# Windowed attention and a mish FFN on one core: unsummed weight pieces stored early, merged q, k and v loads, chunk 2's outputs by SyncE and VectorE

## The chip, the cores and the metric

One core of a Trainium2 chip runs the whole program. The metric is the device time of one execution in microseconds (us), as the median of several runs. Engines are named as the profile names them: PE (TensorE), DVE (VectorE), ACT (ScalarE), POOL (GpSimd) and SP (SyncE, which here issues DMAs only).

## The reference

The kernel computes attention with a window of 64 over 8 sequences of 576 positions with 8 heads of 64 (`scale` is 1/8), puts the heads of a token side by side (`x`, 4608 x 512), and applies a feed-forward layer with `w_in` 512 x 2048, the mish function and `w_out` 2048 x 512.

```python
    scores = scale * np.matmul(q, k.transpose(0, 1, 3, 2))
    pos = np.arange(S)
    rel = pos[:, None] - pos[None, :]
    mask = (rel >= 0) & (rel < window)
    scores = np.where(mask, scores, -1000000000.0)
    scores = scores - np.max(scores, axis=-1, keepdims=True)
    attn = np.exp(scores)
    attn = attn / (np.sum(attn, axis=-1, keepdims=True) + 1e-09)
    return np.matmul(attn, v).astype(np.float32)
...
    h = x @ w_in
    sp = np.where(h > 20.0, h, np.log1p(np.exp(np.minimum(h, 20.0))))
    g = h * np.tanh(sp)
    return (g @ w_out).astype(np.float32)
```

## The kernel before

The tokens are cut into 12 chunks of 384. Heads go in 4 pairs. Every fp32 operand of the feed-forward layer is split into a high and a low fp32r part, and a product is three matmuls (high x high, high x low, low x high). The weights stay in SBUF: `wi` for the first layer, `wo_h` and `wo_l` for the second.

Chunks 0 and 1 run interleaved, step by step, while the weights are loaded and split. Their instructions are held in program order, and at the end of that stage the attention of chunk 2 (`third`) is finished beside them: `third.load(p, "v")` loads a pair's values, `third.values` multiplies them. Chunks 2 and 3 then run plainly, one weight column group `f` after the other. From chunk 4 on the kernel works on two chunks at a time (`Wide`, four of them), with a Strassen-Winograd scheme of seven products on 2 x 2 blocks. It needs weight pieces that are sums of blocks. They are made once, beside chunks 2 and 3, for 8 groups `g`:

- `make_sums(g)` (L794 and on) builds four sums in a tile `w` on DVE (L799, one 128x1024 subtract of blocks of `wi`; L803, four more of 128x256), takes their high part `high` on ACT (L805) and their low part on DVE (L807, `w<-w,high`).
- `keep_sums(g)` (L812 and on) stores what the products need in a DRAM tile `sums`: two unsummed pieces (L815, 128x1024; L816, 128x2x256) and the high and low sums (L820 twice). Each is a DMA on SP's queue, and `after_step` makes it wait for the PE step before it. `load_sums` (L824) reads them back on ACT's queue for the products; the home of `wi` is then reused as a ring.

Meanwhile `wides[0].run(k)` (L852) runs the attention of the first two wide chunks: value products of pair k-1, score products of pair k, then `probs` (masks with maxima on DVE, exponentials on ACT, one multiply and one 32x32 transpose for each half on DVE, 12 moves `pT<-tr` on SP's queue), then the loads of the next pair by `after`: q, k and v for each of the two halves, six DMAs. `fills` (L919) prepares the activation blocks of a `Wide`: four POOL subtracts `t1`, `t2`, `b12`, `t2` again (L925), a high copy on ACT (L916) and a low subtract on DVE (L917) for each of the products. In `pair`, `u3` is copied by ACT (L976) and the sums of products `u` and `t` are made on DVE (L969).

Outputs: `ffn_store` and `out_products` call `store_tile` (L379), which copies a PSUM bank to a tile `o` (L383, on ACT or DVE) and stores it (L388). `o` shares a ring of four homes ("pr") with the softmax tiles and the temporaries of `fills`. For chunk 2, ACT copies tiles 0 and 2 and DVE tile 1; SP stores tile 1, ACT the two others.

SP works through its DMAs in order. A DMA also waits until the one eight issues before it on the same semaphore has landed; SP's and ACT's transfers share these semaphores. The order of PE is written out by the program; the other engines' orders come from a scheduler at build time, within the program's dependences.

In the main loop over the steps `n`, chunk 2's value products and loads stand at the end of chunk 1; a pair's products are followed at once by the load of the pair after next into the same home (`values`, L508):

```python
            if last < n < last + NPAIR:
                third.values(n - last - 1, h_bank)
...
            if last - 2 <= n < last:
                third.load(n - last + 2, "v")
```

Of the kernel before, what the change touches and what calls it, by code (L numbers as in the profile page):

```python
# [29 lines left out]
def tile_window_attn_mish_ffn(  # L30
# [89 lines left out]

    wi = const.tile([P, NF, 2, NC_, P], F32R, name="wi")
# [32 lines left out]
    st_turn, v_turn = itertools.cycle(range(3)), itertools.cycle(range(2))  # L154
# [3 lines left out]

    def v_home(shape, name):
        return ap_.tile(shape, F32, name=name, tag=f"v{next(v_turn)}", bufs=1)  # L160
# [6 lines left out]
    def load_qk(c, p):  # L167
# [13 lines left out]
        q_t = ap_.tile([P, width], F32, name="q_t")  # L181
        k_t = ap_.tile([P, width + BLK], F32, name="k_t", bufs=2)
# [7 lines left out]
    def load_v(c, p):  # L190
# [3 lines left out]
        for at, n, tag in parts:  # L194
            shape = [P, n, P]
            v_t = (mp.tile(shape, F32, name="v_t", tag=tag, bufs={"gh": GHS, "gl": GLS}[tag]) if tag else
                   v_home(shape, "v_t"))
# [3 lines left out]
        return tiles  # L201

# [82 lines left out]
    def run_transpose(pr, pT, n=None):  # L285
        shape = [P, TK // TQ, pr.shape[1], TQ]
        tr = v_home(shape, "tr") if n is None else st_home(shape, F32, "tr", n)
        vec.transpose(tr.rearrange("p k j i -> p j k i"), pr.rearrange("p j (k i) -> p j k i", i=32))
        return pT, each_move(pT, tr)
# [189 lines left out]
    class Att:  # L479
# [7 lines left out]
        def load(self, p, what):  # L487
            a = self
            if p >= NPAIR:
                a, p = (self.next, p - NPAIR) if self.c < PLAIN - 1 else (atts[PLAIN + p - NPAIR], 0)  # L490
# [92 lines left out]
    atts = [Att(c) for c in range(NATT)]  # L583
# [197 lines left out]
    def piece(g, m):  # L781

        def at(first, order="p (l k n) -> p l k n"):
            return ring[:, g % 2, first * PIECE:(first + 1) * PIECE].rearrange(order, l=2, k=2)
# [3 lines left out]
        return at({S2: 2, S3: 3, S4: 4, S1: 5, A22: 6}[m])  # L788
# [5 lines left out]
    def make_sums(g):  # L794
# [12 lines left out]
        nc.vector.tensor_tensor(low, w, high.bitcast(F32), ALU.subtract)  # L807
# [415 lines left out]
```

## Time and profile before

| what | value |
|---|---|
| three runs | 916.98, 918.5, 912.92 us; median 916.98 us |
| profiled execution | 912.17 us, of which the span of the profile is 910.4 us |
| mean granted clock of PE over the span | 0.988 of full speed |
| busy: PE, DVE, ACT, POOL | 874.2, 449.3, 458.5, 219.0 us |
| DMA | 152.04 MB, mean 167 GB/s |

Times in the profile are microseconds from the start of the span. A line such as L383 is a line of the kernel before; where a helper records all operations, it has the helper's line (L82 for what is issued in program order, L129 for every matmul). "<-" between two engines means that the first waited and the second released it. In `out<-in` the first name is the tile written. PE clock is the granted share of full speed, 2.4 GHz; the lower level is 1.2 GHz. The DMA share is the mean busy share of 16 DMA engines. Rows of the profiled execution must be held against its own time, 912.17 us.

### The profile page before, as it was taken

The numbers are of one execution on the slowest core, as the hardware profiler recorded it, in microseconds if no ns is written. First come the engines' busy times: TensorE is split into PE (matmuls) and PEld (weight loads), VectorE is DVE, ScalarE is ACT, GpSimd is POOL, SyncE is SP. The second block draws the span as 40 slices with busy tenths as digits, with TensorE's granted clock in tenths as the row PEclk, the third lists the DMA queues.
The fourth block names the chain that finished last, engine by engine and source line by source line (L and its number), as shares of the span: only waits on it lengthen the run. The fifth ranks groups of instructions, "written<-read, shape, count | busy, mean of one in ns | idle before, by whom it ended". The sixth has DMA issues, their size and how long they took to land.

```text
span 910.4 us, 18898 instructions
## 1 busy us (share of the span) xinstructions
PE 874.2 (96%) x7162; PEld 773.5 (85%) x7162; DVE 449.3 (49%) x1279; ACT 458.5 (50%) x1207; POOL 219.0 (24%) x211
## 2 busy tenths in 40 slices
PE   7899999999979998899998999999999999999998
PEld 5798899888868986789887888887898898989996
DVE  7896888123553657433437524528434334322222
ACT  6866574366653664643555634537535435332322
POOL 4400000021211243212243131234122225232221
PEclk9999999999998998999999999999999999999999
DMA  9553444323588884754653755555656343442401
GB/s 301 176 178 131 160 160 130 105 87 90 180 274 268 280 265 138 237 170 154 193 176 122 252 163 162 181 169 173 200 176 205 127 154 117 158 150 85 133 30 70
DMA packets 97914, 152.04 MB, mean 167 GB/s; under 512 B 9760, under 2 KB 80928, under 8 KB 93728
## 3 DMA queue, kind: packets, MB, share of 16 engines
q1 hardware_dynamic: 83712, 84.57, 29.2%
q10 hardware_dynamic: 14112, 66.26, 21.7%
q8 instruction: 57, 0.93, 0.4%
q14 instruction: 33, 0.27, 0.1%
HBM read 114.88 MB, written 24.12 MB: 153 GB/s over the span
## 4 chain that ended last, share of the span: by engine, by line
PE 83%; DMA 5%; DVE 5%; ACT 3%; SPq 2%; issue 1%; POOL 0%; DVEq 0%; POOLq 0%; ACTq 0%
PE acc L129 39%; PE m_ps L129 24%; PE h_ps L129 13%; PE at L129 3%; DMA k_t<-kT 3%; PE s_ps L129 3%; ACT pr L82 2%; DVE wi L917 1%; SPq L82 1%; PE o_ps L129 1%; DMA out<-o 1%; DVE pr L82 1%; DVE sm L82 1%; DMA wi<-sums 1%; ACT xn L875 0%
## 5 line engine op out<-in xcount | busy, mean ns | idle before, releaser
L129 PE MATMUL acc<-wo_h,gh 128*128 128x512 f32 x576 | 227.4, 399 | 6.6 <-ACT o L383 6.6
L129 PE MATMUL m_ps<-wi 128*128 128x384 f32 x1152 | 223.0, 341 | 9.9 <-ACT u L976 4.3
L129 PE MATMUL acc<-wo_l,gh 128*128 128x512 f32 x576 | 227.0, 394 | 0.0
L129 PEld LDWEIGHTS m_ps<-wi 128*128 128x128 f32 x1152 | 204.4, 189 | 24.0 <-DVE u L969 5.9
L129 PE MATMUL acc<-wo_h,gl 128*128 128x512 f32 x576 | 224.3, 392 | 0.0
L957 POOL TENSOR_TENSOR gl<-t,gh 128x384 fp32r<-128x384 f32 x128 | 131.7, 1030 | 383.5 <-PE m_ps L129 123.2
L129 PE MATMUL h_ps<-xh,wi 128*128 128x384 f32 x512 | 144.0, 343 | 2.2 <-DVE mx L82 1.8
L129 PEld LDWEIGHTS acc<-wo_h,gh 128*128 128x128 f32 x576 | 108.7, 189 | 26.0 <-ACT o L383 7.0
L129 PEld LDWEIGHTS acc<-wo_h,gl 128*128 128x128 f32 x576 | 108.7, 189 | 24.5
L129 PEld LDWEIGHTS acc<-wo_l,gh 128*128 128x128 f32 x576 | 108.8, 189 | 15.4
L82 ACT ACTIVATE pr<-pr,mx 128x96 f32<-128x96 f32 (+1 forms) x288 | 105.5, 372 | 19.5 <-DVE mx L82 19.4
L952 ACT ACTIVATE gh<-t 128x384 fp32r<-128x384 f32 x96 | 50.4, 525 | 125.1 <-DVE t L969 86.2
L969 DVE TENSOR_TENSOR u<-u,m_ps 128x384 f32<-128x384 f32 x64 | 35.3, 552 | 134.6 <-PE m_ps L129 134.6
L129 PEld LDWEIGHTS h_ps<-xh,wi 128*128 128x128 f32 x512 | 95.2, 191 | 6.2 <-issue 2.2
L969 DVE TENSOR_TENSOR t<-u,m_ps 128x384 f32<-128x384 f32 x96 | 53.1, 553 | 84.0 <-PE m_ps L129 84.0
L82 DVE CUSTOM_DVE_ANT_0 pr<-s_ps,masks 128x96 f32<-128x96 f32 (+1 forms) x256 | 49.6, 259 | 79.0 <-PE s_ps L129 78.8
L129 PE MATMUL h_ps<-xl,wi 128*128 128x384 f32 x256 | 87.2, 341 | 0.0
L82 POOL TENSOR_TENSOR gl<-t,gh 128x384 fp32r<-128x384 f32 x32 | 34.9, 1090 | 193.8 <-ACT gh L82 187.8
L82 ACT ACTIVATE t<-h_ps 128x384 f32<-128x384 f32 x64 | 31.4, 491 | 58.5 <-PE h_ps L129 56.2
L1042 DVE TENSOR_TENSOR acc_sb<-acc_sb,acc 128x512 f32<-128x512 f32 x56 | 38.4, 686 | 34.8 <-PE acc L129 34.8
L82 ACT ACTIVATION_READ_ACCUMULATOR pr<-pr,mx 128x1 f32 x288 | 55.1, 191 | 0.0
L953 ACT ACTIVATE t<-t 128x384 f32<-128x384 f32 x96 | 50.2, 525 | 8.8 <-PE m_ps L129 0.5
(70 smaller groups left out, 917.8 us busy)
## 6 DMA issues: line engine op xcount, KB each, us to landing
wi<-sums ACTq DMA_DIRECT2D x32, 1024.0 KB, 5.2
wi<-sums ACTq DMA_DIRECT2D x32, 768.0 KB, 4.5
v_t<-vN SPq DMA_DIRECT2D x46, 384.0 KB, 4.9
k_t<-kT SPq DMA_DIRECT2D x44, 224.0 KB, 5.1
pT<-tr SPq DMA_DIRECT2D x192, 48.0 KB, 3.5
q_t<-qT SPq DMA_DIRECT2D x47, 192.0 KB, 5.2
st<-w_in SPq DMA_DIRECT2D x16, 512.0 KB, 3.5
st<-w_out SPq DMA_DIRECT2D x16, 512.0 KB, 3.6
```

Of the source, the lines that this page charges most:

```text
L82: i = call(*args, **kw)
L129: i = nc.tensor.matmul(*args, **kw)
L917: nc.vector.tensor_tensor(low, b, high.bitcast(F32), ALU.subtract)
L952: nc.scalar.activation(gh, t, AF.Mish)
L953: nc.scalar.activation(t, t, AF.Mish)
L957: nc.gpsimd.tensor_tensor(gl, t, gh.bitcast(F32), ALU.subtract)
L969: nc.vector.tensor_tensor(out_, a, b, ALU.add)
L1042: nc.vector.tensor_tensor(total, total, acc, ALU.add)
```

## The change

Six edits, which leave PE's products as they are:

1. `keep_pieces(g, n)` stores the unsummed pieces for all eight groups in the last steps of chunk 1 (two calls in each of two steps): 4 DMAs of two groups each (128x2x1024) and 8 of 128x2x256, on SP's queue. `keep_sums` keeps its two DMAs for the high and the low sums, whose order in `sums` changes so that rows are twice as long.
2. `q_all`, `k_all` and `v_all` are tiles that stay; the former homes of q, k, v and the transposes `tr` of chunks 0 to 3 are parts of them. `wide_qk` and `wide_v` load both halves of a wide run in one q, one k and one v transfer.
3. The low part of the sums is taken on POOL instead of DVE.
4. Chunk 2's tile 2 is copied by DVE instead of ACT, and SP's queue stores all three tiles.
5. `b12 - b11` of `fills` is taken in place on POOL in `run(2)`; `fills` has two POOL subtracts ahead of its first use (`t2`, `t3`) instead of three.
6. A `Wide`'s output tiles 0 and 3 have a home of their own.

```diff
+    q_all = const.tile([P, 2 * CH], F32, name="q_t")
+    k_all = const.tile([P, 2 * (CH + BLK)], F32, name="k_t")
+    v_all = const.tile([P, 2 * NB, P], F32, name="v_t")
...
+    def wide_qk(c, p):
+        base = bases[c]
+        k_t = k_all[:, :2 * CH + BLK]
+        load.dma_start(q_all, qT[p, :, base:base + 2 * CH])
+        load.dma_start(k_t, kT[p, :, base:base + 2 * CH + BLK])
+        return [(q_all[:, u * CH:(u + 1) * CH], lambda rows, n, w, u=u: k_t[rows, u * CH + n:u * CH + n + w]) for u in range(2)]
+
+    def wide_v(c, p):
+        src = vN[p, bases[c]:, :]
+        load.dma_start(v_all, bass.AP(tensor=vN.tensor, offset=src.offset, ap=[[P, P], [BLK * P, 2 * NB], [1, P]]))
+        return [[v_all[:, u * NB + i, :] for i in range(NB)] for u in range(2)]
...
-    def store_tile(row, acc, by, ending=False, queue=None):
+    def store_tile(row, acc, by, ending=False, queue=None, o=None):
         rows = slice(row, row + P)
-        o = ap_.tile([P, DO], F32, name="o", tag="pr", bufs=PRS)
+        if o is None:
+            o = ap_.tile([P, DO], F32, name="o", tag="pr", bufs=PRS)
...
         for t in range(len(acc)):
-            store_tile(bases[c] + t * P, acc[t], nc.scalar.copy if t in (0, 2) else nc.vector.tensor_copy,
-                       queue=nc.sync if c == 2 and t == 1 else None)
+            third_ = c == 2
+            store_tile(bases[c] + t * P, acc[t], nc.scalar.copy if t == 0 or t == 2 and not third_ else nc.vector.tensor_copy,
+                       queue=nc.sync if third_ else None)
...
-        nc.vector.tensor_tensor(low, w, high.bitcast(F32), ALU.subtract)
+        nc.gpsimd.tensor_tensor(low, w, high.bitcast(F32), ALU.subtract)
...
+    def keep_pieces(g, n):
+
+        after_step(nc.sync.dma_start(
+            sums[g:g + n, :, :2 * PIECE].rearrange("g p n -> p g n"),
+            wi[:, 2 * g:2 * (g + n):2].rearrange("p g l c n -> p g (l c n)").bitcast(F32)))
+        for g in range(g, g + n):
+            after_step(nc.sync.dma_start(sums[g, :, 6 * PIECE:].rearrange("p (l n) -> p l n", l=2),
+                                         wi[:, 2 * g + 1, :, 2:, :].rearrange("p l c n -> p l (c n)").bitcast(F32)))
+
     def keep_sums(g):
-
-        f0, f1 = 2 * g, 2 * g + 1
-        after_step(nc.sync.dma_start(sums[g, :, :2 * PIECE], wi[:, f0].rearrange("p l c n -> p (l c n)").bitcast(F32)))
-        after_step(nc.sync.dma_start(sums[g, :, 6 * PIECE:].rearrange("p (l n) -> p l n", l=2),
-                                     wi[:, f1, :, 2:, :].rearrange("p l c n -> p l (c n)").bitcast(F32)))
         for i, part in enumerate(made.pop(g)):
-            to = sums[g, :, 2 * PIECE:6 * PIECE].rearrange("p (m l n) -> p m l n", m=4, l=2)
-            after_step(nc.sync.dma_start(to[:, :, i, :], part.bitcast(F32)))
+            to = sums[g, :, 2 * PIECE:6 * PIECE].rearrange("p (h l n) -> p h l n", h=2, l=2)
+            after_step(nc.sync.dma_start(to[:, :, i, :], part.rearrange("p (h m) n -> p h (m n)", h=2).bitcast(F32)))
...
+                self.load(k, "v")
+                if k == 2:
+                    b11, b12 = (self.block(0, j) for j in range(2))
+                    nc.gpsimd.tensor_tensor(b12, b12, b11, ALU.subtract)
...
-            t1, t2 = temp("t1"), temp("t2")
-            sub(t1, b12, b11)
+            t2, t3 = temp("t2"), temp("t3")
             sub(t2, b22, t1)
-            sub(b12, b22, b12)
+            sub(t3, t2, b11)
...
+                if t in (0, 3) and "o" not in self.homes:
+                    self.homes["o"] = st_home([P, 2, DO], F32, "o", 1)
...
+        early_pieces = starts[2] // 2 - 3 - n
+        if early_pieces in (0, 1):
+            for g in (0, 2):
+                keep_pieces(4 * (1 - early_pieces) + g, 2)
```

Two places of the order are shown. The first is SP's queue in the last steps of chunk 1, from the last transposed moves of chunk 2 (`pT`) to the first q and k loads of chunk 3; `v_t` are value loads, of chunk 2's pairs 0 to 3 first. Before:

```order
79 L82 DMA pT<-tr 32x192 x12
80 L82 DMA v_t<-vN 128x6x128 x6
81 L82 DMA q_t<-qT 128x384
82 L82 DMA k_t<-kT 128x448
83 L82 DMA pT<-tr 32x192 x12
```

The same place of SP's queue after the change:

```order
79 L82 DMA pT<-v_t 32x192 x12
80 L82 DMA v_t<-vN 128x6x128
81 L838 DMA sums<-wi 128x2x1024
82 L82 DMA v_t<-vN 128x6x128
83 L842 DMA sums<-wi 128x2x256 x2
84 L838 DMA sums<-wi 128x2x1024
85 L842 DMA sums<-wi 128x2x256 x2
86 L838 DMA sums<-wi 128x2x1024
87 L842 DMA sums<-wi 128x2x256 x2
88 L838 DMA sums<-wi 128x2x1024
89 L842 DMA sums<-wi 128x2x256 x2
90 L82 DMA v_t<-vN 128x6x128 x4
```

Twelve stores of unsummed pieces have come between the value loads: pairs 0 and 1 of chunk 2 keep their place, apart from one store, and pairs 2 and 3 stand behind all twelve. (In this listing `tr` has the name `v_t` after the change where it is part of `v_all`.)

The second place is DVE around run 1 of the first `Wide`: the end of run 0 (multiply and transpose), the sums of one group, and the first masks of run 1. Before:

```order
430 L82 TENSOR_TENSOR pr<-pr,sm 128x576
431 L82 STREAM_TRANSPOSE tr<-pr 128x6x3x32
432 L799 TENSOR_TENSOR w<-wi 128x2x2x256
433 L803 TENSOR_TENSOR w<-w 128x256 x4
434 L807 TENSOR_TENSOR w<-w,high 128x1024
435 L82 ISA pr,mx<-s_ps,masks 128x96
436 L82 ISA mx 128x1
```

The same place of DVE after the change:

```order
429 L82 TENSOR_TENSOR pr<-pr,sm 128x576
430 L82 STREAM_TRANSPOSE tr<-pr 128x6x3x32
431 L823 TENSOR_TENSOR w<-wi 128x2x2x256
432 L827 TENSOR_TENSOR w<-w 128x256 x4
433 L823 TENSOR_TENSOR w<-wi 128x2x2x256
434 L82 ISA pr,mx<-s_ps,masks 128x96
435 L82 ISA mx 128x1
```

The low part (L807) has left DVE, and the next group's first subtract (L823, L799 before), which stood behind run 1's masks and the copy of an output tile, has moved ahead of the masks.

## Rows read from the trace of the kernel before

**Rows 1.** Page, part 1: busy us (share of the span) x instructions of each engine.

```profile
PE 874.2 (96%) x7162; PEld 773.5 (85%) x7162; DVE 449.3 (49%) x1279; ACT 458.5 (50%) x1207; POOL 219.0 (24%) x211
```

**Rows 2.** Waits of PE, 225 to 400 us: us in total, times, longest us.

```profile
PE acc L129 <- ACT o L383: 6.6, 1, 6.6
PE m_ps L129 <- ACT u L976: 4.3, 2, 3.2
PE h_ps L129 <- DVE mx L82: 1.8, 1, 1.8
...
PE m_ps L129 <- DVE mx L82: 1.0, 1, 1.0
PE at L129 <- DMA out<-o: 0.9, 1, 0.9
PE at L129 <- DMA pT<-tr: 0.6, 1, 0.6
```

**Rows 3.** Waits of PE, 400 to 910 us, the same columns.

```profile
PE m_ps L129 <- DVE u L969: 3.3, 5, 0.9
PE m_ps L129 <- DVE t L969: 3.0, 2, 1.5
```

**Rows 4.** Windows of 10 us: us; busy PE, PEld, DVE, ACT, POOL; clock, DMA share, GB/s.

```profile
160.00:170.00 10.00, 10.00 (x89) 8.76 (x89) 2.74 (x5) 3.15 (x7) 0.00 (x0) 1.00 0.39 125
...
260.00:270.00 10.00, 6.65 (x87) 5.51 (x75) 5.32 (x31) 5.64 (x27) 0.00 (x0) 1.00 1.06 359
270.00:280.00 10.00, 6.76 (x23) 6.19 (x24) 4.46 (x9) 4.45 (x7) 1.22 (x2) 0.66 0.75 256
...
290.00:300.00 10.00, 8.18 (x35) 6.97 (x32) 6.95 (x34) 9.10 (x30) 0.00 (x0) 0.83 1.06 367
...
350.00:360.00 10.00, 6.74 (x20) 5.43 (x19) 7.17 (x7) 2.18 (x4) 3.66 (x3) 0.66 0.29 89
```

**Rows 5.** Timeline of SP, 255 to 276 us: start, us, what it issues.

```profile
258.00 0.71 SPq L820 DMA_DIRECT2D sums<-w  x1
```

**Rows 6.** Timeline of DVE, 250 to 276 us: start, us, instruction, idle before, releaser.

```profile
260.72 0.26 DVE L82 CUSTOM_DVE_ANT_0 pr<-s_ps,masks 128x96 f32<-128x96 f32 x1 [3.46 <-PE s_ps L129]
...
267.50 1.23 DVE L799 TENSOR_TENSOR w<-wi 128x1024 f32<-128x1024 f32 x1 [3.96 <-DMA sums<-w]
```

**Rows 7.** Timeline of ACT, 155 to 186 us, the same columns.

```profile
156.02 0.49 ACT L82 ACTIVATE t<-h_ps 128x384 f32<-128x384 f32 x1 [1.44 <-PE h_ps L129]
```

**Rows 8.** Timeline of PE, 140 to 200 us, values of chunk 2's pair 2.

```profile
170.55 0.92 PE L129 MATMUL o_ps<-pT,v_t 128*64 128x64 f32 x24
```

**Rows 9.** Windows of 5 us, columns as in rows 4.

```profile
295.00:300.00 5.00, 5.00 (x19) 4.51 (x18) 3.14 (x11) 4.97 (x22) 0.00 (x0) 0.66 1.08 396
...
315.00:320.00 5.00, 5.00 (x26) 4.50 (x25) 5.00 (x25) 4.42 (x18) 0.00 (x0) 1.00 1.02 319
```

**Rows 10.** DMA issues, 145 to 200 us: KB each, median us to landing.

```profile
v_t<-vN SPq DMA_DIRECT2D x6, 384.0 KB, 3.4
```

**Rows 11.** Timeline of ACT, 262 to 275 us: start, us, instruction, idle before, releaser.

```profile
270.54 1.28 ACT L82 ACT_TABLE_LOAD   x1 [3.87 <-DMA v_t<-vN]
...
272.59 0.59 ACT L383 COPY o<-acc 128x512 f32<-128x512 f32 x1
```

**Rows 12.** POOL's instructions by line and form: busy us, mean ns; idle before.

```profile
L925 POOL TENSOR_TENSOR t<-xn 128x768 f32<-128x768 f32 x4 | 7.3, 1827 | 0.0
```

**Rows 13.** Timeline of ACT, 345 to 377 us.

```profile
353.82 0.48 ACT L976 COPY u<-m_ps 128x384 f32<-128x384 f32 x1 [1.77 <-DVE w L807]
```

**Rows 14.** Timeline of DVE, 338 to 377 us.

```profile
349.40 2.41 DVE L82 TENSOR_TENSOR pr<-pr,sm 128x576 f32<-128x576 f32 x1
351.73 2.02 DVE L807 TENSOR_TENSOR w<-w,high 128x1024 fp32r<-128x1024 f32 x1
...
373.58 0.76 DVE L82 TENSOR_TENSOR pr<-pr,sm 128x576 f32<-128x576 f32 x1
```

**Rows 15.** Timeline of POOL, 336 to 377 us.

```profile
348.62 2.56 POOL L925 TENSOR_TENSOR t<-xn,t 128x768 f32<-128x768 f32 x1 [1.63 <-DVE wi L917]
```

More of the change, by code (lines that the diff above doesn't have):

```diff
@@ L152, in at_set @@
         return ps_at.tile([P, DO], F32, name=name, tag=f"at{n}")
-    st_turn, v_turn = itertools.cycle(range(3)), itertools.cycle(range(2))
+    st_turn, q_turn, v_turn = (itertools.cycle(range(n)) for n in (3, 2, 2))
     def st_home(shape, dtype, name, n=None):
         return mp.tile(shape, dtype, name=name, tag=f"st{next(st_turn) if n is None else n}", bufs=1)
-    def v_home(shape, name):
-        return ap_.tile(shape, F32, name=name, tag=f"v{next(v_turn)}", bufs=1)
     def in_steps(c, p):
@@ L180, in load_qk @@
             return q_t, keys
-        q_t = ap_.tile([P, width], F32, name="q_t")
-        k_t = ap_.tile([P, width + BLK], F32, name="k_t", bufs=2)
+        i = next(q_turn)
+        q_t = q_all[:, i * CH:(i + 1) * CH]
+        k_t = k_all[:, i * (CH + BLK):(i + 1) * (CH + BLK)]
         first = c == 0 and p < 2
@@ L195, in load_v @@
             shape = [P, n, P]
-            v_t = (mp.tile(shape, F32, name="v_t", tag=tag, bufs={"gh": GHS, "gl": GLS}[tag]) if tag else
-                   v_home(shape, "v_t"))
+            if tag:
+                v_t = mp.tile(shape, F32, name="v_t", tag=tag, bufs={"gh": GHS, "gl": GLS}[tag])
+            else:
+                i = next(v_turn)
+                v_t = v_all[:, i * NB:(i + 1) * NB, :]
             load.dma_start(v_t, bass.AP(tensor=vN.tensor, offset=src.offset + at * BLK * P,
@@ L489, in load @@
             if p >= NPAIR:
-                a, p = (self.next, p - NPAIR) if self.c < PLAIN - 1 else (atts[PLAIN + p - NPAIR], 0)
+                a, p = self.next, p - NPAIR
+                if self.c == PLAIN - 1:
+                    if p == 1:
+                        wides[0].load(0, what)
+                    return
             if a:
@@ L581, in tile_window_attn_mish_ffn @@
     steps += [(c, f) for c in range(2, PLAIN) for f in range(NF)]
-    atts = [Att(c) for c in range(NATT)]
+    atts = [Att(c) for c in range(PLAIN)]
     for a, b in zip(atts, atts[1:]):
@@ L787, in piece @@
             return both[:, :, m == A12]
-        return at({S2: 2, S3: 3, S4: 4, S1: 5, A22: 6}[m])
+        if m == A22:
+            return ring[:, g % 2, 6 * PIECE:].rearrange("p (l k n) -> p l k n", l=2, k=2)
+        i = (S2, S3, S4, S1).index(m)
+        two = ring[:, g % 2, (2 + i // 2 * 2) * PIECE:(4 + i // 2 * 2) * PIECE]
+        return two.rearrange("p (l m k n) -> p l m k n", l=2, m=2, k=2)[:, :, i % 2]
     def after_step(i):
@@ L856, in run @@
             if k >= 1:
-                for u, a in enumerate(self.atts):
-                    value_products(a.v[k - 1], a.pT.pop(k - 1), [at[u][:, n:n + BLK] for n in range(0, CH, BLK)])
+                moves = self.pT.pop(k - 1)
+                for u in range(2):
+                    value_products(self.v[k - 1][u], (pT_all[:, :, u], moves), [at[u][:, n:n + BLK] for n in range(0, CH, BLK)])
             if scored:
@@ L861, in run @@
                 s_ps = {}
-                for u, a in enumerate(scored.atts):
+                for u in range(2):
                     for m in range(NM):
@@ L900, in probs, with load @@
                                                 tr[r:r + TQ, i].rearrange("p u j q -> p (u j q)")))
-            for u, a in enumerate(self.atts):
-                a.pT[k] = pT_all[:, :, u], moves
-                self.after(u, k, "qk")
-        def after(self, u, k, what):
-            if k + 1 < NPAIR:
-                self.atts[u].load(k + 1, what)
-            elif self.next:
-                self.next.atts[u].load(0, what)
+            self.pT[k] = moves
+            self.load(k + 1, "qk")
+        def load(self, k, what):
+            a, k = (self, k) if k < NPAIR else (self.next, 0)
+            if a:
+                getattr(a, what)[k] = {"qk": wide_qk, "v": wide_v}[what](a.cs[0], k)
         def block(self, i, j):
```

22 lines of the change are left out of this document (10 added, 12 removed).

## The prediction

> **What bounds the kernel now.** I read the page first, then PE's waits, then the timelines around each wait. PE is busy for 96% of the span [rows 1], so only two things can move the time: stretches in which PE stands still, and stretches in which it runs at the lower of its two clock levels. The change removes no matmul. The waits between 225 and 400 us [rows 2] sum to some 15 us, and the longest is 6.6 us, for ACT's copy of an output tile. Behind 400 us some 6 us more are spent in front of `m_ps` [rows 3].
>
> The clock adds to it. Between 270 and 280 us the granted clock was 0.66, between 290 and 300 us 0.83, between 350 and 360 us 0.66 [rows 4], each time just behind a stall. A mean of 0.66 is 68% of the time at the half level (1.2 instead of 2.4 GHz): 0.68 x 6.76 us busy = 4.6 us at half speed, 2.3 us lost. By the same working 290 to 300 us lost 0.34 x 8.18 / 2 = 1.4 us, and 350 to 360 us 2.3 us. So a stall of several us costs about 2 us more than its length.
>
> **The early pieces: a new wait.** Twelve stores now stand on SP's queue at the end of chunk 1: 4 of 1.05 MB and 8 of 0.26 MB, 6.29 MB. Before, SP issued the six value loads of chunks 2 and 3 there with nothing between them. Now the loads of pairs 2 and 3 of chunk 2 stand behind all twelve stores. DMA engines have time in that stretch, since their share was 0.39 between 160 and 170 us [rows 4]. But one queue moves its bytes in order: the store of `w` issued at 258.00 us released VectorE only at 267.50 us [rows 5, 6], with other stores and a part of the loads ahead of it.
>
> PE takes pair 2's values at 170.55 us [rows 8]. The first store waits for a step of PE that ends at about 156 us, where ACT takes its `h_ps` [rows 7], so bytes start to move at about 157 us. Up to and including pair 2's load stand 6.29 + 2 x 0.39 = 7.07 MB, and 7.86 MB if chunk 0's three output tiles (0.26 MB each, ACT's queue) share the engines before it. Engines that were full moved 319 to 396 GB/s [rows 9], and 359 GB/s over 260 to 270 us [rows 4]. The fixed part of a landing is 3.4 us [rows 10] less 1.3 us for 0.39 MB at 300 GB/s, 2.1 us. Best: 157 + 7.07/0.396 + 2.1 = 177.0 us, a stall of 6.4 us. Worst: 157 + 7.86/0.319 + 2.1 = 183.7 us, 13.2 us. At 359 GB/s it is 8.3 us without and 10.5 us with the outputs ahead; I take 9.0. Such a stall brought 2.3 us of half clock at 270 us. **Cost: 11.3 us (8 to 16).** What queues behind it: the next activations on ACT stand behind output transfers that wait for stores to land, and PE's steps behind them, but those transfers wait no longer than pair 2's values do, so I count nothing more.
>
> In exchange SP is spared 16 stores between 242 and 332 us, and the six loads at each wide run become three. I count that inside the waits below, since no row shows SP itself holding PE there except 0.6 us at the transposed moves [rows 2].
>
> **Chunk 2's outputs: the 6.6 us.** ACT stood behind its output transfer until `v_t` had landed, 3.87 us, then loaded a table (1.28 us) and copied two activations before it reached the third tile at 272.59 us [rows 11]. Now SP stores, and VectorE copies the third tile, behind one multiply and one transpose, each some 0.76 us [rows 14], after the last exponential (270.54 - 3.87 = 266.67 us [rows 11]). The copy ends at about 268.9 us, so a stall of about 2.2 us stays: gain 4.4 us. A stall that short at 292 us still brought 1.4 us of half clock, so I count 1.2 of the 2.3 us. Against that, VectorE's next piece sum (`w<-wi`) now stands ahead of run 1's masks and waits for the store of the last sum, as it waited 3.96 us in before, behind them [rows 6]. The masks began at 260.72 us. That store was issued at 258.00 us [rows 5]; with POOL's longer subtract (below) it is issued some 1.2 us later, and lands, at the 3.4 us of rows 10, at 262.3 to 262.6 us if less stands ahead of it. With the sum's own 1.23 us the masks are late by 0 to 3.1 us; I take 1.0 us for PE. Net gain 4.6 us (minus 3.1 to 8.9).
>
> **The low part of the sums on POOL.** It takes 1.23 us of VectorE eight times; on POOL the nearest row is 1.83 us for 768 columns [rows 12], so 1024 columns take about 2.4 us. VectorE is freed ahead of run 2's masks, where PE waited 1.8 us [rows 2] and lost 1.4 us of clock: I take 2.4 of these 3.2 us (0 to 3.2).
>
> At the change to the first `Wide`, ACT's `u` copy waited for VectorE's subtract [rows 13], whose tile shares the home, and PE waited for `u`. The subtract ran from 351.73 us and took 2.02 us [rows 14], since it stood behind a multiply stretched by POOL. On POOL it would end at about 352.2 us. That stretch holds 6.2 us of waits (4.3 for `u`, 1.0 for `mx`, 0.9 for `out<-o`) [rows 2] and 2.3 us of half clock. I take 4.0 us (0 to 8.5).
>
> POOL's work beside VectorE has a price that speaks against this part: a multiply of 0.76 us took 2.41 us beside POOL's subtract [rows 14, 15], 1.65 us more, and POOL's own took 2.56 instead of 1.83 us. The Trainium skill (SBUF — State Buffer, section "Who interferes with whom") says that a VectorE operation with two SBUF inputs and a GpSimd operation that reads SBUF exclude each other, and that the later of the two waits until the first is done. The trace agrees: the multiply that began at 349.40 us ended at 351.81 us, 0.63 us after POOL's subtract ended at 351.18 us. By that rule each moved subtract can hold VectorE for up to its own length; by the row alone the price is 1.65 us a collision. It is rival 2.
>
> **Fills and the own output home.** Each fill has one POOL subtract fewer (1.83 us) at its start, and tiles 0 and 3 no longer wait for a home of the softmax ring. The waits in the three later transitions sum to 6.3 us [rows 3], of which I take about half, 3.3 us (0 to 6.3).
>
> **Sum.** Gains 4.6 + 2.4 + 4.0 + 3.3 = 14.3 us; cost 11.3 us; net minus 3.0 us. The profiled execution took 912.17 us (span 910.4), so 909.2 us; it lies 4.8 us under the median of the three runs, 916.98, so against that median I expect 914 us. By the ends of the terms the net goes from minus 18 (all 26.9 us of gains, the least cost, 8.4 us of which 6.4 are the stall and 2.0 its clock) to plus 19 (no gain, masks 3.1 us late, 15.5 us of cost).
>
> **Rivals.**
> 1. *The value loads are not late.* If loads pass the stores, or the stores drain before 170 us, only the gains stay: minus 14.3 us, 903 us. For it: engines at 0.39 share [rows 4]. Against it: 7.07 MB in the 11.5 us from 157 to 168.5 us would need 615 GB/s, and no full stretch shows over 396 [rows 9].
> 2. *POOL against VectorE, slower.* The eight subtracts fall beside the multiplies of runs 0 to 4, and the chain masks, exponentials, multiply, transposes, moves gets later. Once already PE waited for its end (0.6 us for `pT<-tr` [rows 2]), so there is little slack. One collision in each of four runs costs 1.65 us and some 1.5 us of half clock: 12.6 us on top of minus 3.0, plus 9.6 us, 927 us. It decides from a slack under 1.65 us. Against it: POOL is free most of that stretch, and VectorE gets 1.23 us back a sum.
> 3. *The gains do not come.* Another wait of the same run ends as late as the removed one (the table load, the moves, the masks), and only a third of the gains is left: 11.3 - 4.8 = plus 6.5 us, 923 us. For it: the chains of ACT and VectorE in 260 to 275 us are long whatever the copy does. Against it: the 3.87 us on ACT are spent on nothing but a transfer [rows 11].
>
> **How the numbers follow.** Forecast 0.42, rival 1 0.25, rival 2 0.17, rival 3 0.16. The forecast's own range is 908 to 921. About 1% (9.2 us) is what a measurement of this kernel can tell from no change. Faster by more: nearly all of rival 1 and a little of the forecast, 0.31. Slower by more (over 926): two thirds of rival 2, some of rival 3 and the forecast's tail, 0.19. The rest, 0.50, is within 1%. The range that leaves out one in ten on either side is 899 to 927 us.
>
> **What would show it.** Right: a new wait of PE in front of chunk 2's `o_ps` at about 170 us, of 6 to 13 us, released by `v_t<-vN`; a granted clock near 0.66 behind it; the 6.6 us at 266 us down to 2 or 3; no wait for `u` over 2 us near 351 us; waits before `m_ps` behind 400 us at about half. Wrong: no wait at 170 us (rival 1), new waits on `pT<-tr` or `mx` between 250 and 335 us with VectorE's multiplies over 2 us (rival 2), or the wait at 266 us still over 5 us, with another releaser (rival 3).

## The result and the profile after

The changed kernel took 925.95 us (median of 12 runs, 919.96 to 930.8) against 915.52 us for the kernel before (12 runs, 912.71 to 919.68): a ratio of 1.011, with a 95% interval of 1.0081 to 1.014. It is slower by some 10 us. The forecast was 914 us, a little faster than before; the time lies inside the stated range (899 to 927 us), but on the other side of no change.

The profiled execution took 927.89 us (span 926.1 us, mean granted clock 0.980, against 910.4 us and 0.988). The waits of PE between 165 and 235 us in the changed kernel, in the columns of [rows 2] (before, that stretch has none):

```profile
PE o_ps L132 <- issue: 9.7, 1, 9.7
```

And its waits of PE between 235 and 405 us, the largest and the least:

```profile
PE at L132 <- issue: 5.6, 1, 5.6
PE m_ps L132 <- ACT u L1005: 4.4, 2, 3.1
PE h_ps L132 <- DVE mx L82: 3.5, 1, 3.5
PE m_ps L132 <- DVE u L998: 1.1, 1, 1.1
...
PE at L132 <- DMA pT<-tr: 0.3, 1, 0.3
```

"issue" as a releaser means that the profile shows nothing that the engine waited for. The wait of 6.6 us for the output tile [rows 2] is gone. But 9.7 us have come in front of chunk 2's values (`o_ps`), 5.6 us in front of run 2's values (`at`), and the wait for `mx` has grown from 1.8 to 3.5 us; the wait for `u` is as long as it was. All waits of this view sum to 18.7 us between 235 and 405 us; in the kernel before it was 16.4 us. Behind 405 us they sum to 4.8 us instead of 6.3 us [rows 3]:

```profile
PE m_ps L132 <- DVE t L998: 3.1, 2, 1.6
PE m_ps L132 <- DVE u L998: 1.2, 2, 0.6
PE m_ps L132 <- ACT u L1005: 0.5, 2, 0.3
```

The windows of 10 us around the new wait, columns as in [rows 4], show the engines of the DMA full and the clock falling:

```profile
160.00:170.00 10.00, 10.00 (x89) 8.59 (x88) 2.74 (x5) 3.14 (x7) 0.00 (x0) 1.00 1.04 375
170.00:180.00 10.00, 0.87 (x6) 0.55 (x4) 0.56 (x1) 1.46 (x3) 0.00 (x0) 0.77 1.03 340
180.00:190.00 10.00, 9.40 (x72) 7.80 (x73) 1.12 (x2) 0.96 (x2) 0.00 (x0) 0.72 0.34 104
```

Over 165 to 235 us the mean clock was 0.93 with PE busy for 60.28 us, so 0.07 x 60.28 = 4.2 us were lost; before it was 1.00 there. The two profiled spans differ by 15.7 us. The parts are 9.7 us of new wait, 4.2 us of clock behind it, 2.3 us more waits and 1.4 us more half clock between 235 and 405 us, less 1.5 us of waits behind that and 0.5 us at the start. The clock is given to two digits, so each part that comes from it is known to within about 1 us. The medians differ by 10.4 us: the profiled execution of before, 912.17 us, is near the low end of its runs, that of after in the upper half of its own.

### The profile page after: what moved, and what is told of

Same layout as the page of the kernel before. It is cut to its first block, busy times and chain, and to the rows that moved or that the text cites. A ratio compares the mean times of both kernels' runs of the same rounds, so it can differ in the third digit from the quotient of the medians.

```text
span 926.1 us, 18789 instructions
## 1 busy us (share of the span) xinstructions
PE 879.9 (95%) x7162; PEld 777.8 (84%) x7162; DVE 444.0 (48%) x1272; ACT 458.4 (50%) x1206; POOL 238.9 (26%) x219
## 5 line engine op out<-in xcount | busy, mean ns | idle before, releaser
L132 PEld LDWEIGHTS acc<-wo_h,gh 128*128 128x128 f32 x576 | 109.1, 190 | 19.5 <-issue 0.3
L132 PEld LDWEIGHTS acc<-wo_l,gh 128*128 128x128 f32 x576 | 109.6, 190 | 15.7
```

Source lines behind the costliest of these rows:

```text
L132: i = nc.tensor.matmul(*args, **kw)
```

## Where the new wait comes from

SP's timeline of the changed kernel, 150 to 200 us, from the third of the large stores on:

```profile
163.55 1.25 SPq L838 DMA_DIRECT2D sums<-wi  x1
164.84 2.53 SPq L842 DMA_DIRECT2D sums<-wi  x2
167.42 1.29 SPq L838 DMA_DIRECT2D sums<-wi  x1
168.76 2.58 SPq L842 DMA_DIRECT2D sums<-wi  x2
171.43 15.84 SPq L82 DMA_DIRECT2D v_t<-vN  x4
```

PE's timeline there, the first product after the wait:

```profile
180.59 1.55 PE L132 MATMUL o_ps<-pT,v_t 128*64 128x64 f32 x24 [9.72 <-issue]
```

SP reached pair 2's value load only at 171.43 us, when the last store was issued. The view of DMA issues (KB each, us to landing) for 171.4 to 172 us shows how long that load then took:

```profile
v_t<-vN SPq DMA_DIRECT2D x1, 384.0 KB, 9.0
```

So the values were there at 180.6 us, within the bounds of the prediction's working (177 to 184 us). Whether the stores are the cause, and whether it is their place in the queue or the load on the engines, four kernels tell.

**e1: the early stores undone.** The pieces are stored again by `keep_sums`; all else is as changed.

```diff
     def keep_sums(g):
+        f0, f1 = 2 * g, 2 * g + 1
+        after_step(nc.sync.dma_start(sums[g, :, :2 * PIECE], wi[:, f0].rearrange("p l c n -> p (l c n)").bitcast(F32)))
+        after_step(nc.sync.dma_start(sums[g, :, 6 * PIECE:].rearrange("p (l n) -> p l n", l=2),
+                                     wi[:, f1, :, 2:, :].rearrange("p l c n -> p l (c n)").bitcast(F32)))
...
-        if early_pieces in (0, 1):
-            for g in (0, 2):
-                keep_pieces(4 * (1 - early_pieces) + g, 2)
```

> The changed kernel with its early pieces undone: the unsummed pieces are stored again in keep_sums, between 242 and 332 us; all else as changed. Theory (the stores on SP's queue make chunk 2's values late): the 9.7 us wait in front of o_ps and its half clock go, 12 us less than the changed kernel's 925.95, so 914 us or a little more, since 6.3 MB come back beside the wide runs. Rival (POOL's subtracts and VectorE's collisions cost the time, and the stall at 170 us is made good later): under 4 us less, 922 us or more.

Measured: 911.43 us, 0.9938 of before (0.9916 to 0.996), and no wait of PE between 100 and 235 us. So the early stores cost 14.5 us by the medians, and what is left of the change (the other five edits and the new order of rows in `sums`) is a gain of about 0.6%. The theory holds; the rival falls.

**e2: the same stores in chunk 2.**

```diff
-        early_pieces = starts[2] // 2 - 3 - n
-        if early_pieces in (0, 1):
-            for g in (0, 2):
-                keep_pieces(4 * (1 - early_pieces) + g, 2)
+        late_pieces = n - starts[2] // 2 - 1
+        if late_pieces in (0, 2, 4, 6):
+            keep_pieces(late_pieces, 2)
```

> The changed kernel with the early pieces stored in the first steps of chunk 2 (behind all value loads, one call in every second step) instead of at the end of chunk 1. Theory: the wait in front of o_ps is gone and nothing comes back beside the wide runs, 12 us less than the changed kernel, 912 to 914 us; the waits of 3.5 us (mx) and 5.6 us (at) between 270 and 310 us stay. Rival (the stores cost wherever they stand): a new wait of 3 us or more in chunk 2, and no more than 6 us less than the changed kernel.

Measured: 917.77 us (909.96 to 921.49), 0.9996 (0.9964 to 1.0028). The 9.7 us are gone; 2.6 us of waits stand in chunk 2 in their place (1.9 us, released by nothing the profile shows, and 0.7 us for `tr`). Its runs scatter over 11.5 us, those of e1 over 2, and the median lies between the two expectations. The trace is that of the fastest run, 909.96 us, so the waits of the slower ones are not seen; what makes them scatter was not found.

**f1: the same stores at the same steps, on POOL's queue.**

```diff
-        after_step(nc.sync.dma_start(
+        after_step(nc.gpsimd.dma_start(
...
-            after_step(nc.sync.dma_start(sums[g, :, 6 * PIECE:].rearrange("p (l n) -> p l n", l=2),
+            after_step(nc.gpsimd.dma_start(sums[g, :, 6 * PIECE:].rearrange("p (l n) -> p l n", l=2),
```

> The changed kernel with the twelve early stores at the same steps, but issued on POOL's queue instead of SP's. Theory (pair 2's values are late because they stand behind the stores in one queue): the loads share the engines packet by packet and pass most of the stores, the 9.7 us wait in front of o_ps falls under 4 us, and the time is 6 us or more below the changed kernel's 925.95. Rival (the DMA engines as a whole are too slow for 6.3 MB there, whatever the queue): a wait of 7 us or more stays and the time is within 4 us of the changed kernel.

Measured: 910.46 us, 0.9958 (0.9937 to 0.9979), no wait between 100 and 235 us. Its windows of 10 us, columns as above:

```profile
160.00:170.00 10.00, 10.00 (x89) 8.59 (x88) 2.75 (x5) 3.15 (x7) 3.28 (x5) 1.00 1.02 349
170.00:180.00 10.00, 10.00 (x90) 8.58 (x89) 1.59 (x3) 3.02 (x7) 3.26 (x5) 1.00 1.06 368
```

Its PE timeline, pair 2's values:

```profile
170.85 0.92 PE L132 MATMUL o_ps<-pT,v_t 128*64 128x64 f32 x24
```

SP's timeline in it, 160 to 162 us, the load of pair 2's values, and the DMA issues of the same stretch:

```profile
161.34 0.37 SPq L82 DMA_DIRECT2D v_t<-vN  x1
```

```profile
v_t<-vN SPq DMA_DIRECT2D x1, 384.0 KB, 4.6
```

The DMA engines were as full as in the changed kernel (349 and 368 GB/s against 375 and 340), and pair 2's values were in time. So it is the place behind the stores in one queue that made them late, not the load on the engines: worth some 15 us of 926.

The delay has two parts. SP issued the load at 161.34 us here and at 171.43 us in the changed kernel, 10.1 us later, because SP first had to issue the stores, which took it 0.9 to 1.3 us each, where a load alone took 0.37 us. Once issued, the load took 9.0 us to land instead of 4.6 us. The Trainium skill (DMA: Bandwidth & Descriptors, section "Queues, rings and completion order") says that each DMA engine takes the entries of one queue in order and takes turns between the queues by packets. The second part agrees with that; it does not explain the first. The Trainium skill (DMA: Bandwidth & Descriptors, section "Rules for kernel authors") says that spreading transfers over the issuing engines does not help bandwidth and only saves time of issuing. The first part agrees with that: the rate hardly changed, and the load was issued 10.1 us earlier. f1 takes away both parts at once, so no run shows which of them alone would have made PE wait. It also spread the stores out, since POOL issued the last of them at 178.30 us and SP by 171.3 us.

**f2: half of the stores early, half in chunk 2.**

```diff
         if early_pieces in (0, 1):
-            for g in (0, 2):
-                keep_pieces(4 * (1 - early_pieces) + g, 2)
+            keep_pieces(2 * (1 - early_pieces), 2)
+        if early_pieces in (-4, -6):
+            keep_pieces(-early_pieces, 2)
```

> The changed kernel with half of the early stores (groups 0 to 3, 3.15 MB) at the end of chunk 1 and the other half in chunk 2. Theory: 3.15 MB less ahead of pair 2's values are 8.8 us at the 359 GB/s of a full stretch, so the 9.7 us wait falls to about 1 us (0 to 3), and the time to that of e2_pieces_late, 918 us or below. Rival (a wait that does not go by bytes but by the queue's waits for landings): 5 us or more of the wait stay.

Measured: 911.22 us, 0.9961 (0.9934 to 0.9987), no wait between 100 and 235 us. SP issued pair 2's load 7.2 us after the first store (15.2 us in the changed kernel), and it took 6.0 us to land (9.0 us): 11 us earlier, where the theory had 8.8 us from the bytes. The wait goes by how much stands ahead; since half the bytes are also half the stores, f2 does not tell the two apart.

## Where the gains went

**e3: chunk 2's outputs alone, in the kernel before.**

```diff
-            store_tile(bases[c] + t * P, acc[t], nc.scalar.copy if t in (0, 2) else nc.vector.tensor_copy,
-                       queue=nc.sync if c == 2 and t == 1 else None)
+            third_ = c == 2
+            store_tile(bases[c] + t * P, acc[t], nc.scalar.copy if t == 0 or t == 2 and not third_ else nc.vector.tensor_copy,
+                       queue=nc.sync if third_ else None)
```

> The kernel before with the edit on chunk 2's outputs alone (VectorE copies tile 2, SP stores all three). Theory (the chain from run 1's masks to the last move is longer than PE's work up to run 2, and the 6.6 us wait only covered that): the wait for o falls to 2 or 3 us, a wait of 3 to 5 us for the moves or masks of run 2 comes in its place, and the time is within 3 us of before. Rival (the wait is lost time, as the prediction took it): 5 to 8 us faster than before.

Measured: 916.76 us, 1.0006 (0.9984 to 1.0027): nothing. The time is the theory's, and so is the new wait for the moves (4.5 us), but the wait for `o` did not shrink; it only has another releaser. PE's waits of 235 to 405 us in this kernel:

```profile
PE acc L129 <- DVE o L383: 6.6, 1, 6.6
PE at L129 <- DMA pT<-tr: 4.5, 1, 4.5
PE h_ps L129 <- DVE mx L82: 2.4, 1, 2.4
```

VectorE's timeline in it, 255 to 276 us:

```profile
267.57 1.23 DVE L800 TENSOR_TENSOR w<-wi 128x1024 f32<-128x1024 f32 x1 [4.06 <-DMA sums<-w]
268.72 0.16 DVE L82 TENSOR_SCALAR sm<-sm 128x6 f32<-128x6 f32 x1
...
272.45 0.68 DVE L383 COPY o<-acc 128x512 f32<-128x512 f32 x1
```

VectorE stood until 267.57 us in front of the first subtract of the next group's sum, waiting for the store of the last sum's low part to land, as it did before (267.50 us [rows 6]). The copy of `o` came behind it in VectorE's order, at 272.45 us; ACT's copy had come at 272.59 us [rows 11]. So ACT's 3.87 us behind the output transfer and VectorE's 3.96 us behind the store were two waits side by side, on two chains that reach the copy of `o` within 0.14 us of each other, and taking one away showed the other.

In the changed kernel the scheduler had moved that subtract ahead of run 1's masks. VectorE's timeline there:

```profile
276.35 1.23 DVE L823 TENSOR_TENSOR w<-wi 128x1024 f32<-128x1024 f32 x1 [10.25 <-DMA sums<-w]
...
284.95 2.51 DVE L82 TENSOR_TENSOR pr<-pr,sm 128x576 f32<-128x576 f32 x1
```

PE's timeline of the changed kernel, the two products behind its waits:

```profile
278.94 0.66 PE L132 MATMUL h_ps<-xh,wi 128*128 128x384 f32 x1 [3.50 <-DVE mx L82]
...
302.89 2.83 PE L132 MATMUL at<-pT,v_t 128*64 128x64 f32 x48 [5.57 <-issue]
```

The last score of run 1 was done at 273.15 us, but VectorE waited for a landing until 276.35 us (10.25 us idle), and PE, which needs the banks that the masks read, stood for 3.5 us. The masks' lateness and a multiply of 2.51 us beside POOL's subtract (284.44 to 286.83 us) then held back the moves, which SP issued from 288.30 to 296.73 us. The 5.6 us in front of run 2's values came at their end. The DMA issues of 296.5 to 297 us show it, a reload of pieces, a store and the last move:

```profile
wi<-sums ACTq DMA_DIRECT2D x1, 1024.0 KB, 6.3
sums<-w SPq DMA_DIRECT2D x1, 512.0 KB, 7.0
pT<-tr SPq DMA_DIRECT2D x1, 48.0 KB, 6.6
```

The moves issued between 294 and 296 us landed in 1.9 us; the last one, beside the reload of 1 MB, took 6.6 us, to about 302.7 us, and PE went on at 302.89 us. Seven more kernels looked at that chain. A measure of it is the interval from the last score of run 1 to the first value product of run 2, and the same from run 2 to 3. In the kernel before they are 26.3 and 21.4 us, in the changed one 29.7 and 21.5 us; from run 0 to 1 of the kernel before, where PE never waits, it is 17.6 us.

**e5: the masks first.** As e2, and the first subtract of the third, fifth and seventh group waits for its run's last mask.

```diff
+        if g % 2 == 0 and "mask" in made:
+            tc.add_manual_dep(first.ins, made["mask"].name, SYNC, reason="masks first")
...
-    sums_at = [(begin + k // 2 * every + (-3, 1, 1, 5)[i + k % 2 * 2], fn, k)
+    sums_at = [(begin + k // 2 * every + (0 if k else -3, 1, 1, 5)[i + k % 2 * 2], fn, k)
```

> As e2_pieces_late, and the first subtract of the third, fifth and seventh group's sums is made to stand behind the masks of its run. Theory: the 3.5 us wait for mx goes, and the 5.6 us wait in front of run 2's values shrinks, as the masks' lateness (3.5 us) was part of it: 4 to 8 us less than e2_pieces_late. Rival (POOL beside the multiply and the reload of pieces beside the moves make that wait): the mx wait goes but the at wait stays at 5 us or more, 2 to 4 us less.

Measured: 912.61 us (910.38 to 913.98), 0.9966 (0.9946 to 0.9986); intervals 24.0 and 22.4 us. No wait for `mx` in front of `h_ps`, but 4.2 us for `o`, since the subtract now stands ahead of that copy, and 2.9 us for `pT<-tr`. By the medians 5.2 us less than e2; with e2's scatter this is weak evidence. **g3: the same on f1.** The diff is that of e5, on f1's early stores on POOL's queue.

> f1_pool_queue (early stores on POOL's queue) with the masks ahead of the next sum as in e5_masks_first. If the two do not touch each other: the 4.3 us wait for mx of f1_pool_queue goes, 2 to 4 us less than its 910.5 us. If the wait only changes its place: within 2 us of it.

Measured: 910.41 us, 0.9943 (0.9925 to 0.9962), against 910.46 us for f1. The 4.3 us for `mx` of f1 are gone and 4.6 us for `o` have come: the wait changed its place.

**f4: no wait for the landing.** e1, with the transfer of the low sums reading unsummed weights (the low parts are left out of the sums).

```diff
-        for i, part in enumerate(made.pop(g)):
+        high, _ = made.pop(g)
+        for i, part in enumerate((high, wi[:, f1].rearrange("p l c n -> p (l c) n").rearrange("p (m a) n -> p m (a n)", m=4))):
```

> e1_pieces_back, where the transfer that stored the low sums reads the unsummed weights instead (same bytes; the low parts in the sums are left out), so that the next group's first subtract no longer waits for a store to land. Theory: that wait held VectorE, and behind it the copy of chunk 2's output tile: the 6.5 us wait for o falls to 3 us or less and the time by 3 to 7 us under e1_pieces_back's 911.4 us. Rival (run 1's own chain of exponentials, multiply and transposes is as long): the wait stays over 5 us, or comes back in front of run 2's values, and the time is within 2 us.

Measured: 912.22 us, 0.9978 (0.9961 to 0.9994), against 911.43 us for e1. The wait for `o` is gone altogether, 6.5 us in e1, and the time did not fall. PE's waits of 235 to 405 us:

```profile
PE s_ps L132 <- ACT gh L82: 8.8, 2, 5.1
PE at L132 <- DMA sums<-wi: 4.0, 1, 4.0
PE at L132 <- DMA pT<-tr: 1.9, 1, 1.9
```

The first interval is 29.3 us, longer than e1's 25.9 us. The time is the one that the expectation's rival gave, but not its mechanism (run 1's own chain of exponentials, multiply and transposes): VectorE finished run 1's transposes at 269.3 us, early, but SP issued the moves from 274.19 us on and took 11.13 us for them (8.43 us in the changed kernel's run 1). The larger part of the wait for `gh` (5.1 of 8.8 us) hangs on the same moves. ACT's timeline, 268 to 290 us:

```profile
284.88 0.49 ACT L82 ACTIVATE t<-h_ps 128x384 f32<-128x384 f32 x1 [6.74 <-DMA pT<-tr]
```

ACT stood 6.74 us until moves had landed; it issued a reload of pieces at 284.45 us, just before it went on, and PE waited 5.1 us for what ACT wrote next.

**g1: no sums' work at all.** e1, with `make_sums` empty and both transfers of `keep_sums` reading unsummed weights. The sums are left out; the bytes and their places stay.

```diff
     def make_sums(g):
-        f0, f1 = 2 * g, 2 * g + 1
...
+        pass
```

> e1_pieces_back without the work of the sums on VectorE, ACT and POOL: keep_sums stores unsummed weights in their place (the same bytes at the same places of SP's queue; the sums are left out). It parts what the engines' sums cost from what their stores cost. Between run 1's last score and run 2's first value lie 17.6 us of PE's own work; in the kernel before that interval is 26.3 us, in e1_pieces_back 25.9 us, and from run 2 to run 3 it is 21.4 and 21.2 us. If the work on VectorE, ACT and POOL holds the chain: both intervals fall to 17.6 to 19 us and the time to 900 us or less. If the stores do (landings, SP's queue): the intervals stay over 21 us, the time at 907 us or more.

Measured: 909.22 us, 0.9937 (0.9915 to 0.9958); intervals 29.3 and 19.4 us. VectorE, ACT and POOL are free of the sums, and run 2's values are 9.7 us late nonetheless. SP's timeline of 262 to 300 us, the moves:

```profile
272.22 11.86 SPq L82 DMA_DIRECT2D pT<-tr  x12
```

The DMA issues of that stretch in g1 (KB each, median us to landing):

```profile
sums<-wi SPq DMA_DIRECT2D x9, 512.0 KB, 7.7
...
k_t<-kT SPq DMA_DIRECT2D x2, 416.0 KB, 6.5
...
pT<-tr SPq DMA_DIRECT2D x12, 48.0 KB, 5.7
```

The moves are 48 KB each and took 5.7 us to land, and 11.86 us to issue, behind 512 KB stores and loads that took 6 to 8 us. The last transpose had ended at 269.7 us.

**g2: neither sums nor stores.** As g1, with all stores in the first steps of chunk 2 (the sums are left out).

```diff
+        if late_pieces in (1, 3, 5, 7):
+            for g in (late_pieces - 1, late_pieces):
...
+                    after_step(nc.sync.dma_start(to[:, :, i, :], part.rearrange("p (h m) n -> p h (m n)", h=2).bitcast(F32)))
...
     def keep_sums(g):
...
+        pass
```

> As g1_no_sums_work, with all stores (pieces and what stands for the sums) moved to the first steps of chunk 2, so that beside the wide runs neither the sums' work nor their stores stand. If the runs' own chain (masks, exponentials, multiply, transposes, moves) is the bound: waits of 5 us or more stay between run 1 and run 3. If the sums and their traffic are: both intervals at 17.6 to 18.5 us, the waits between 235 and 405 us under 5 us, and the time 12 us or more below the kernel before, 902 us or less.

Measured: 921.82 us, 1.0066 (1.0046 to 1.0086). The time says nothing of the runs, because the 14.7 MB of stores, now all in chunk 2, made 12.6 us of waits for moves there (`pT<-tr`), the same fault at another place. The intervals do: 24.3 us from run 1 to 2, still, but 17.4 us from run 2 to 3 and 17.8 us from run 3 to 4. So without the sums and their stores PE never waits between runs 2 and 4. Between runs 1 and 2 it waits once, 3.5 us for `o`, and VectorE's timeline there (276 to 300 us) shows why:

```profile
292.65 0.69 DVE L400 COPY o<-acc 128x512 f32<-128x512 f32 x1 [2.94 <-DMA out<-o]
```

VectorE's copy of the third output tile waited until an earlier output had been stored. PE's clock over that interval was 0.86 with 20.76 us busy, so 2.9 us more were lost. Together that is 6.4 of the 6.9 us by which the first interval exceeds the second.

**h1: the reloads later.** g3, with the first four reloads made to wait for their steps.

```diff
             for part in LOADS:
-                load_sums(f - 7, part)
+                after_step(load_sums(f - 7, part))
```

> g3_pool_queue_masks_first, with the four reloads of the first pieces (ACT's queue, 3.7 MB, issued between 257 and 300 us, in the middle of runs 1 and 2) made to wait for the steps of chunk 3 at which the program asks for them. If these reloads hold the moves and loads of runs 1 and 2 back: the intervals from run 1 to 2 and 2 to 3 fall from 24.6 and 21.9 us to 21 and 19 us or less, and the time by 4 us or more from 910.4 us. If they do not: within 2 us, or slower, where the first products of the wide stage wait for the reload.

Measured: 914.14 us, 0.9992 (0.9978 to 1.0007); intervals 24.4 and 25.5 us, against 24.6 and 21.9 us in g3. The reloads taken away from run 1 did not shorten the first interval, and the second grew. So in g3's order they are not what holds run 1.

**g4: the sums behind the chain.** f1, with that first subtract behind the run's last transpose.

```diff
-                vec.transpose(tr[:, :, u].rearrange("p k j i -> p j k i"), units[u][0].rearrange("p j (k i) -> p j k i", i=32))
+                made["mask"] = vec.transpose(tr[:, :, u].rearrange("p k j i -> p j k i"), units[u][0].rearrange("p j (k i) -> p j k i", i=32)).ins
```

> f1_pool_queue with the first sum of each run's window (third, fifth and seventh group) behind the run's last transpose instead of ahead of its masks, so that VectorE never waits for a store inside the chain of masks, copy of o, multiply and transposes. If that wait is what makes runs 1 to 3 late: no wait for mx or o over 2 us, the two intervals together 42 us or less (46.9 in f1_pool_queue), 904 to 908 us. Against it: the sums end later, and the wait for u near 351 us grows by what is gained; then 909 to 912 us.

Measured: 920.64 us, 1.0059 (1.0038 to 1.008), slower than both times of the expectation. The first interval fell to 19.5 us (20.9 us in f1), the next two were 25.4 and 24.0 us, and the wait for `u` grew to 11.7 us (4.0 us in f1): what was gained early came back late, and more.

**f3, h2 and h3: the other parts.** f3 is e1 with the low part of the sums back on VectorE (the first diff). h2 is the kernel before with that part on POOL as its only edit (the same two lines the other way round). h3 is the kernel before with the edits on the fills and on the output home alone (the second diff, its core).

```diff
-        nc.gpsimd.tensor_tensor(low, w, high.bitcast(F32), ALU.subtract)
+        nc.vector.tensor_tensor(low, w, high.bitcast(F32), ALU.subtract)
```

```diff
-            t1, t2 = temp("t1"), temp("t2")
-            sub(t1, b12, b11)
+            t2, t3 = temp("t2"), temp("t3")
             sub(t2, b22, t1)
-            sub(b12, b22, b12)
+            sub(t3, t2, b11)
...
+                           o=self.homes["o"][:, t // 3, :] if t in (0, 3) else None)
```

> e1_pieces_back with the low part of the sums back on VectorE. Theory (the chains of run 1 and 2 are held by the landing of the sums' stores, not by who subtracts): within 3 us of e1_pieces_back's 911.4 us, and the wait for u near 351 us stays at 3 us or more. Rival 2 of the prediction (POOL's subtract stretches VectorE's multiplies on the chain): 4 us or more faster than e1_pieces_back. The prediction's own gain for this part (6.4 us): that much slower.

> The kernel before with the low part of the sums on POOL as the only edit. f3_low_on_dve lies about 0.5% (4 to 5 us) above e1_pieces_back; if that part is a gain by itself: 3 to 6 us faster than before. If it was only worth something together with the other edits: within 2 us of before.

> The kernel before with the edits on fills (b12 - b11 on POOL in run 2, two subtracts ahead) and the own output home of a Wide alone. The prediction took 3.3 us for them; the waits behind 400 us fell by 1.2 to 1.5 us in all kernels with these edits, so 1 to 2 us faster than before, which is within the noise of a comparison.

Measured: f3 914.53 us, 0.9991 (0.9974 to 1.0009); h2 916.24 us, 1.0018 (1.0002 to 1.0034); h3 910.37 us, 0.9953 (0.9937 to 0.9968). So POOL's subtract alone is a loss of some 2 us, barely clear of none, and a gain of 3 us by the medians (0.5% by the ratios of f3 and e1) beside the other edits; why the company matters is not shown. The fills and the home are the one part tried that is a gain by itself: 4 us, twice what was expected. The waits behind 405 us show 1.5 us of it (6.3 us before, 4.8 us in h3). The mean granted clock of its runs is 0.9911, against 0.9885 in the runs of the kernel before that were taken with them, which at 874 us busy is an estimated 2 us more; which stall is spared was not found. The merged loads of q, k and v were not tried alone.

Why the wait for `u` stayed can be read in the changed kernel. POOL's timeline around it:

```profile
365.50 2.24 POOL L955 TENSOR_TENSOR t<-xn,t 128x768 f32<-128x768 f32 x1 [0.96 <-DVE wi L947]
367.71 3.05 POOL L831 TENSOR_TENSOR w<-w,high 128x1024 fp32r<-128x1024 f32 x1
```

ACT's timeline, the copy of `u`:

```profile
370.79 0.48 ACT L1005 COPY u<-m_ps 128x384 f32<-128x384 f32 x1 [2.19 <-POOL w L831]
```

The subtract on POOL stood behind the fills' own subtract, which waited for VectorE, and took 3.05 us beside VectorE's subtract (366.65 to 368.56 us) instead of 2.38 us alone; ACT's copy came right behind it and waited 2.19 us, as it had waited 1.77 us for VectorE's [rows 13]. In f3, with the subtract back on VectorE, the view shows 1.6 us for `u` instead of 4.1 us in e1 (the expectation had it stay at 3 us or more), but 6.5 instead of 2.9 us for the moves.

## Why the prediction was wrong, point by point

The step that failed is the price of the gains. Chunk 2's outputs and the low part on POOL were taken as 4.6 + 6.4 = 11.0 us; in e1, where both are in, little or nothing is left of it beyond what the fills and the home give alone (some 4 us in e1 and in h3).

- **The early pieces.** Right in place, and nearly in size: the wait was 9.7 us (taken 9.0, bounds 6.4 to 13.2); the trace names no releaser for it ("issue"), e1, f1 and f2 do. The half clock behind it was 4.2 us (taken 2.3). Together 13.9 us against 11.3 us; by undoing them 14.5 us. The mechanism was half of it: the prediction counted the bytes ahead of the load, and in the trace 10.1 us of the delay came before SP issued the load at all. (The 300 GB/s in its fixed part of a landing stands in no row; with the rows' 319 GB/s that part would be 2.2 us instead of 2.1 us.)
- **Chunk 2's outputs.** The step was "VectorE copies the third tile, behind one multiply and one transpose". It left out what else stood ahead in VectorE's order: the subtract of the next sum, with its wait for a store. The row for it was in the prediction (267.50 us, 3.96 us idle [rows 6]) and was used only for the masks. A gain of 4.6 us was taken; alone (e3) it was 0.
- **The masks behind that subtract.** Foreseen, with bounds of 0 to 3.1 us late, and sized too small: PE waited 3.5 us where 1.0 us was taken, and the lateness went on into the moves of run 2, where PE waited 5.6 us more (the last move beside a reload), which the sum did not follow.
- **The low part on POOL.** 6.4 us were taken; it is a loss of some 2 us alone and a gain of some 3 us in company. The step "on POOL it would end at about 352.2 us" took POOL to be free. It stood behind the fills' own subtract, and PE's wait for `u` was 4.4 us where it had been 4.3 us.
- **Fills and own home.** 3.3 us taken, 4 us measured (h3). The number came out, the reason only in part: the waits that were to halve fell by 1.5 us, and the rest was not foreseen.
- **The sum.** Gains of 14.3 us became some 4 us (e1), the cost 11.3 us became 14.5 us; minus 3.0 became plus 10.4. Of the rivals the second gave nearly the right total (927 us), by luck, since its mechanism was not the main one: a collision with POOL is there (2.51 us for a multiply), but the same subtract on POOL costs only some 2 us by itself (h2). The third, gains that do not come because another wait ends as late, is what e3 and f4 show, with 923 us.
- The deeper error is one of method: each wait of the stretch from 250 to 380 us was priced as if the others would stay, yet they share one chain of masks, copies, moves and landings. With one of its waits taken away or moved (e3, f4, g3, g4), the waits of 235 to 405 us stayed at 14 us or more, and the time did not fall beyond the noise.

Still open: whether SP's late issue or the order of the bytes behind it would alone have made PE wait at 170 us, what scatters e2's runs, and where most of h3's gain comes from. Of the versions that leave nothing out, e1 (0.9938), g3 (0.9943), h3 (0.9953), f1 (0.9958), f2 (0.9961) and e5 (0.9966) are faster than both kernels; their intervals overlap, so their order is not shown.

## What to carry to other kernels

Before bulk stores go into a "free" stretch, list the loads that the same queue issues behind them and give each its due time; here the bytes ahead divided by the rate of a full stretch gave the new wait to within 1 us, and another queue, or half the bytes, removed it. Before a wait is counted as a gain, read what the instruction that takes its place stands behind on its own engine, in the order after the change: here the two waits ahead of the copy of `o` were on chains that ended within a microsecond of each other, and taking away ACT's gave nothing (e3). Where several waits lie on one repeated chain, price the chain from end to end.

## What the runs showed of the hardware

The place in a queue mattered more than the load on the engines: with engines at 349 and 368 GB/s, loads on another queue than the stores came in time (f1), and behind the same stores in one queue PE waited 9.7 us for them. Of the load's delay, 10.1 us passed before SP issued it. A move of 48 KB, which landed in a median of 2.0 us over 250 to 345 us of the changed kernel, took 5.7 us among half-megabyte transfers (g1). A stall of 9.7 us cost 4.2 us more by the clock (165 to 235 us of the changed kernel), where 2.3 us were lost behind the one of 6.6 us before [rows 4].
